# Attention and a top-1 mixture of experts in one Trainium2 kernel: gathered tokens take the same way through DVE's block transposes and DRAM as the hidden blocks

## Chip, cores and metric

The kernel runs on one core of one Trainium2 chip. The metric is the device time of one execution in microseconds (us); the number quoted for a kernel is the median of its runs.

## What is computed

The reference is a block-causal attention over 8 batches, 8 heads, 576 positions and head size 64 (blocks of 64; a query sees its own block and the earlier ones), whose output is laid out as x, 4608 tokens of 512. A gate matrix picks one of 8 experts for each token:

```python
logits = x @ w_gate
expert_idx = np.argmax(logits, axis=1)
gate_w = probs[np.arange(N), expert_idx]
for e in range(E):
    xe = x[expert_idx == e]
    h = np.maximum(xe @ w1[e], 0.0)      # 512 -> 1024
    out[expert_idx == e] = gate_w[...] * (h @ w2[e])   # 1024 -> 512
```

All data are float32. This change lies in the expert part alone.

## The kernel before

Attention runs first, and its tokens are written to a DRAM table `xd` (512 values and the gate weight in each row). The expert part then works in **slots** of 128 tokens that share an expert. With these inputs there are 38 slots (0 to 37), and the seven experts that get any tokens take 7, 9, 1, 4, 2, 3 and 12 of them, in this order: expert changes fall at slots 7, 16, 17, 21, 23 and 26. Slots 0 to 2 (`EARLY` = 3) are prepared specially; `period(t)` writes out the work of slot t from 2 on.

To keep float32's precision, TensorE multiplies in pieces: every operand is split into a high part (rounded, `xh`, `hh`, first half of `w`) and a low part (the rest, `xl`, `hl`), and a product is high*high + low*high + high*low. So `first_pe(t)` is 24 matmuls (two halves f of the 1024 hidden columns, 12 each), and `second_pe(t)` 24 more. PE's order in `period(t)` is `first_pe(t)`, the transposes of the next tokens (`rows_in(t + 1)`), `second_pe(t - 2)`.

- **Tokens.** `gather(t + 2)` (POOL, L881) fetches 128 rows by index into one of five buffers `xg`. `rows_in` (L899) turns them with four TensorE transposes into PSUM bank `px`; `rows_act` (L909, L912) has ACT copy `px` twice, as `xh` and `xf`, and `rows_pool` (L918) subtracts them to `xl`. There is one `xh` and one `xl`, so they may be written only when `first_pe(t)` is through.
- **Hidden blocks.** `relu_act` (L978) takes PSUM `ph` to `h`. `blocks` (L1015) has DVE transpose the 32 x 32 blocks of `h` into `hblk`; `leave` (L1022, a DMA issued by ACT) writes `hblk` to a DRAM buffer `there`, and `enter` (L1033, four DMAs) reads it back in another order, which completes the transpose, into `hp` (shown as `high` in the profile). `split_act` (L1044) makes `hh`, `split_pool` (L1054, two instructions) `hl`. These feed `second_pe` two periods later.
- **Weights.** SyncE loads the next expert's weights in eight chunks of 512 KB into four buffers `raw` (L1251, eight per expert), and DVE makes high and low parts from each: `units` (L1229 the high part, L1232 the low part). A table `pk`, worked out on the chip by `pieces`, says which of the four pieces (two chunks each, two CASTs and two subtractions) belong to a slot: an expert of one slot has all four of its successor's pieces in it, one of two slots has three and one, one of three has two, one and one, and longer ones have one in each of the first four slots. Pieces 0 and 1 (w1) run in period t, 2 and 3 (w2) in period t + 1. The weight memory holds two experts.
- **Order.** Each engine works through its own list, waiting on semaphores. In `period(t)` DVE has `blocks(t, 0)`, `blocks(t, 1)`, `units(t - 1, 1)`, `units(t, 0)`. ACT has `out_act`, `enter(t - 1)`, the two ReLUs, the two copies of `px`, `leave(t)`, `split_act(t - 1)`. `out_act` (L1100) scales by the gate weight, `out_pool` (L1106) scatters rows to the output.

## Time and profile before

| what | us |
| --- | --- |
| median of 3 runs (lowest, highest) | 847.27 (847.0, 852.77) |
| the profiled execution | 846.09 |
| its span, first to last instruction | 844.3 |
| outside the span | 1.8 |

Times in the profile count from the span's start. The expert part runs from about 377 us to the end. PE is TensorE's matmuls, PEld its weight loads, DVE VectorE, ACT ScalarE, POOL GpSimd, SP SyncE; ACTq and SPq are the queues' own instructions, among them the DMA issues. L-numbers are lines of the kernel before. first(17) stands for `first_pe(17)`, second(17) for `second_pe(17)`, hh(17) for the high part of slot 17's hidden block.

### The profile page before, as it was taken

To read this page: it belongs to the slowest core of one execution; us is meant where nothing else is said; L and a number is where in the kernel's file an instruction comes from. 1 tells how busy PE (TensorE), PEld (TensorE's weight loads), DVE (VectorE), ACT (ScalarE), POOL (GpSimd) and SP (SyncE) were. 2 spreads that over 40 slices of the span, in tenths; PEclk is the share of its full clock that TensorE was granted. 3 is DMA by queue.
4 is the path that set the end of the run, shared out by engine and by line. 5 is a ranking of instruction groups with operands and counts; after the bars stand their busy time and mean duration, and the time that the engine had idled before them with its cause. 6 is when DMAs were issued, how large, how long until landed. Compare 5 with 4: busy or idle time off the path is not lost.

```text
span 844.3 us, 16283 instructions
## 1 busy us (share of the span) xinstructions
PE 802.0 (95%) x4656; PEld 604.5 (72%) x4656; DVE 434.2 (51%) x1217; ACT 419.4 (50%) x1049; POOL 395.5 (47%) x394
## 2 busy tenths in 40 slices
PE   4999999999999999989999999989999999999993
PEld 2666677766666666667778888867788778888872
DVE  3567676767666667748445443135657771111100
ACT  3777677777777777734233333232232233333321
POOL 4112244434344623343666655553566575554452
PEclk9999999999999999999999999999999999999997
DMA  5229735455443538142466755446869854344440
GB/s 180 71 98 184 198 116 133 132 126 149 119 137 119 122 105 230 34 119 92 162 207 227 245 195 181 142 131 211 271 211 288 278 181 138 127 150 145 131 133 36
DMA packets 69248, 132.03 MB, mean 156 GB/s; under 512 B 10257, under 2 KB 31505, under 8 KB 69138
## 3 DMA queue, kind: packets, MB, share of 16 engines
q1 hardware_dynamic: 36418, 74.06, 30.8%
q10 hardware_dynamic: 25200, 36.71, 13.3%
q0 software_dynamic: 7520, 19.97, 7.2%
q8 instruction: 47, 0.77, 0.4%
q14 instruction: 63, 0.52, 0.2%
HBM read 90.91 MB, written 40.33 MB: 155 GB/s over the span
## 4 chain that ended last, share of the span: by engine, by line
PE 83%; issue 4%; DVE 4%; DMA 3%; POOL 2%; ACT 2%; DVEq 1%; ACTq 0%; POOLq 0%; SPq 0%
PE py L1083 21%; PE o L270 12%; PE ph L940 10%; PE o L940 10%; PE ya L169 7%; PE xa L169 4%; PE o L305 4%; PE px L899 1%; DMA raw<-w 1%; DMA there<-hblk 1%; PE o L299 1%; ACT pb L200 1%; PE o L158 1%; DVE w L1232 1%; POOL xl L918 0%
## 5 line engine op out<-in xcount | busy, mean ns | idle before, releaser
L1083 PE MATMUL py<-w,low 128*128 (+1 forms) x912 | 223.0, 399 | 1.7 <-issue 0.9
L1083 PEld LDWEIGHTS py<-w,low 128*128 128x128 f32 x912 | 168.1, 188 | 41.3 <-POOL low L1054 1.9
L1015 DVE STREAM_TRANSPOSE hblk<-h 128x512 f32<-128x512 f32 x70 | 48.9, 706 | 216.0 <-ACT h L978 135.3
L112 POOL TENSOR_SCALAR q<-qd 128x640 f32<-128x640 f32 x32 | 57.9, 1809 | 189.5 <-PE o L158 115.8
L1054 POOL TENSOR_TENSOR low<-high,low 128x512 fp32r<-128x512 f32 x70 | 101.8, 1474 | 32.1 <-ACT low L1044 32.1
L918 POOL TENSOR_TENSOR xl<-xf,xh 128x512 fp32r<-128x512 f32 x38 | 49.9, 1313 | 83.7 <-ACT xf L912 83.3
L940 PE MATMUL ph<-w,xh 128*128 x280 | 77.0, 397 | 6.1 <-DVE w L1229 4.2
L940 PE MATMUL o<-w,xh 128*128 x280 | 75.5, 391 | 0.0
L200 ACT ACTIVATE pb<-ya,neg 128x320 f32<-128x320 f32 (+2 forms) x96 | 50.0, 524 | 48.0 <-DVE neg L185 48.0
L1100 ACT ACTIVATE y<-py,xg 128x512 f32<-128x512 f32 x38 | 26.1, 686 | 92.8 <-PE py L1083 88.0
L1232 DVE TENSOR_TENSOR w<-raw,w 128x1024 f32 x48 | 70.1, 1499 | 0.0
L1106 POOL DMA_INDIRECT out<-y,idx x35 | 42.7, 1221 | 52.9 <-ACT y L1100 42.8
L978 ACT ACTIVATE h<-ph 128x512 f32<-128x512 f32 x37 | 22.1, 598 | 91.1 <-issue 52.4
L940 PEld LDWEIGHTS ph<-w,xh 128*128 128x128 f32 x280 | 53.0, 190 | 19.2 <-issue 7.2
L1229 DVE CAST w<-raw 128x1024 f32 x48 | 49.1, 1060 | 30.5 <-issue 22.2
L169 PE MATMUL ya<-kd,q 64*128 64x192 f32 (+2 forms) x192 | 61.8, 457 | 2.7 <-ACT pb L200 2.7
L169 PE MATMUL yb<-kd,q 64*128 64x192 f32 (+2 forms) x192 | 61.8, 456 | 0.0
L940 PEld LDWEIGHTS o<-w,xh 128*128 128x128 f32 x280 | 52.6, 188 | 11.4
L1044 ACT CAST low<-high 128x1024 fp32r<-128x1024 f32 x35 | 36.7, 1050 | 44.8 <-DVE hblk L1015 21.2
L697 POOL DMA_INDIRECT tab<-toks,posi x40 | 41.7, 1042 | 27.3 <-DVE run L664 13.8
L978 ACT ACTIVATE h<-o 128x512 f32<-128x512 f32 x37 | 22.1, 598 | 59.8 <-PE o L940 59.8
L200 ACT ACTIVATE pb<-yb,neg 128x192 f32<-128x192 f32 (+2 forms) x96 | 49.7, 525 | 0.4 <-DVE neg L185 0.4
(977 smaller groups left out, 1742.2 us busy)
## 6 DMA issues: line engine op xcount, KB each, us to landing
raw<-w SPq DMA_DIRECT2D x52, 512.0 KB
there<-hblk ACTq DMA_DIRECT2D x35, 512.0 KB, 3.1
high<-there ACTq DMA_DIRECT2D x140, 128.0 KB
qd<-qT SPq DMA_DIRECT2D x32, 352.0 KB, 3.2
v<-vt SPq DMA_DIRECT2D x32, 352.0 KB, 7.5
kd<-kT SPq DMA_DIRECT2D x32, 288.0 KB, 4.2
xd<-xt SPq DMA_DIRECT2D x7, 1026.0 KB
xd<-xg SPq DMA_DIRECT2D x9, 256.5 KB, 11.2
```

What stands on the lines that cost most here:

```text
L112: self.nc.gpsimd.tensor_scalar(q, self.raws[m][0][:, 0 : 512 + P], 0.125, None, ALU.mult)
L169: ins = mm(out, q[r, 128 * (i - 1) : 128 * i], k[r, o : o + n], start=True, stop=True, skip_group_check=True)
L200: ins = self.nc.scalar.activation(dst, src, AF.Exp, bias=self.neg[m][:, c : c + 1], scale=1.0, accum_out=self.sums[m][:, c : c + 1])
L270: self.nc.tensor.matmul(out[r], self.raws[m][2][:, slot], self.ph[m, bank][:, c0:c1], start=t in (0, 5), stop=t in (4, 5), skip_group_chec ...
L918: pool.tensor_sub(self.xl, self.xf, self.xh).then_inc(sem["xp"], 1)
L940: m = pe.matmul(self.ph[f], x[:, P * k : P * k + P], weights(k, f, part), start=start and k == 0, stop=stop and k == 3,)
L978: act.activation(self.h[f], self.ph[f], AF.Relu).then_inc(sem["ra"], 1)
L1015: dve.transpose(self.ht.rearrange("p (b f c i) -> p f c b i", b=4, f=2, c=4)[:, f], self.h[f].rearrange("p (c b j) -> p c b j", c=4, b=4), ...
L1054: pool.tensor_sub(self.hl[t % 2][:, f].rearrange("p (c a i) -> p c a i", c=4, a=4), inner(t)[:, f], self.hh[t % 2][:, f].rearrange("p (c a ...
L1083: m = pe.matmul(self.py[t % 2], h[:, c // 4, P * (c % 4) : P * (c % 4) + P], wf[:, bass.ds(off + (base + 512 * c), 512)], start=n == 0, st ...
L1229: dve.tensor_copy(part(c, 0), raw[c % 4]).then_inc(sem["wh"], 1)
L1232: dve.tensor_sub(part(c, 1), raw[c % 4], part(c, 0)).then_inc(sem["wd"], 1)
```

## The change

From slot 6 on (`EARLY + AHEAD`, with `AHEAD` = 3) the tokens no longer go through TensorE. DVE transposes the 32 x 32 blocks of slot t + 3's tokens into a third part of `hblk` along with slot t's hidden blocks; `there`, `hblk` and `hp` grow from 1024 to 1536 columns, and the DMAs carry 768 KB each way. On the far side ACT makes `xh` from `hp` (`apart_act`), POOL `xl` (`rows_pool`); the second copy `xf` is gone. Within `hblk` and `hp` the twelve column groups are now interleaved (a step of 12 elements, 48 bytes, between neighbours of a group), where a run of 32 neighbours was contiguous before. `xh`, `xl` and the PSUM banks `ph` are double (even slots use what were `pt0` and `pt1`); ReLU writes back into its PSUM bank and DVE reads it there. Six token buffers replace five, tokens are gathered four periods ahead instead of two, and the gate weight is copied out by DVE (`gates`), since the buffer is reused before the output is scaled. In a slot DVE now does its weight pieces first and the blocks afterwards, except where a new bit in `pk` ("late": position 0 or 1 within the expert's slots, and three or four pieces up to this slot) puts the blocks ahead. In the last slot DVE takes one of the two `hl` halves. In the start, `pieces` moves behind the first weight work, and `rows_pool(3)` ahead of `out_pool(0)`.

```diff
-XG = 5
+XG = 6
+AHEAD = 3
...
+        do(v.tensor_scalar(c[2], c[2], 1.0, None, ALU.is_le))
+        do(v.tensor_scalar(c[2], c[6], 2.5, c[2], ALU.is_gt, ALU.mult))
+        do(v.scalar_tensor_tensor(c[7], c[7], 2.0, c[2], ALU.mult, ALU.add))
...
+    def phs(self, t):
+        return self.pt if t > EARLY and t % 2 == 0 else self.ph
...
+        def apart_act(t):
+            act.wait_ge(sem["dr"], 64 * (t - AHEAD - EARLY + 1))
+            rows_free(act, t)
+            r, (xh, _) = apart(t)
+            act.copy(xh, r).then_inc(sem["xa"], 2)
...
-            act.activation(self.h[f], self.ph[f], AF.Relu).then_inc(sem["ra"], 1)
+            ph = self.phs(t)[f]
+            act.activation(self.h[f] if t < EARLY else ph, ph, AF.Relu).then_inc(sem["ra"], 1)
...
-            dve.transpose(
-                self.ht.rearrange("p (b f c i) -> p f c b i", b=4, f=2, c=4)[:, f],
-                self.h[f].rearrange("p (c b j) -> p c b j", c=4, b=4),
-            ).then_inc(sem["tb"], 1)
+            to = self.ht.rearrange("p (b i g) -> p g b i", b=4, g=12)
+            u = t + AHEAD
+            if u < NS:
+                dve.wait_ge(sg[u % XG], 16 * gathered(u))
+                rows = self.xg[u % XG]
+                dve.transpose(to[:, 8:12], rows[:, 0:DM].rearrange("p (k b j) -> p k b j", k=4, b=4)).then_inc(
+                    sem["tb"], 1
+                )
...
+            for f in range(2):
+                dve.wait_ge(sem["ra"], 2 * t + f - 1)
+                dve.transpose(
+                    to[:, 4 * f : 4 * f + 4], self.phs(t)[f].rearrange("p (c b j) -> p c b j", c=4, b=4)
+                ).then_inc(sem["tb"], 1)
...
+                if t + 1 < NS:
+                    act.wait_ge(sem["xp"], t + 1)
...
+            elif more and t + 1 >= EARLY + AHEAD:
+                apart_act(t + 1)
+            if more:
+                rows_pool(t + 1)
...
-            if more:
-                rows_in(t + 1)
-                rows_act(t + 1)
-                rows_pool(t + 1)
+            work(t)
             leave(t)
...
+        def work(t, old=True):
+            late = units(t - 1, 1, t) if old else None
+            units(t, 0)
+            if old:
+                with dve.If(late < 1):
+                    blocks(t)
+                dve.end_ifs()
```

DVE's list around slot 18 of the kernel before: the two block transposes, then the load of `pk` that opens the pieces, with their branches (`raw` and `w` are the weights).

```order
L1015 STREAM_TRANSPOSE hblk<-h_4962 128x4x4x32
L1015 STREAM_TRANSPOSE hblk<-h_4963 128x4x4x32
L1214 TENSOR_LOAD pk
L1214 ISA x2
L1221 REGISTER_ALU x3
L1221 COMPARE_AND_BRANCH
```

The same slot now opens with `pk`, and a branch on the late bit may put three transposes (tokens `xg`, then the two PSUM banks) and the gate's copy there; then come the pieces (left out).

```order
L1285 TENSOR_LOAD pk
L1285 ISA x2
L1294 REGISTER_ALU x2
L1294 COMPARE_AND_BRANCH
L1066 STREAM_TRANSPOSE hblk<-xg_194 128x4x128
L1072 COPY gates<-xg_194 128x1
L1078 STREAM_TRANSPOSE hblk<-pt_4967 128x4x128
L1078 STREAM_TRANSPOSE hblk<-pt_4968 128x4x128
L1294 UNCONDITIONAL_BRANCH
L1297 REGISTER_ALU x3
L1297 COMPARE_AND_BRANCH
```

Without the bit the same four instructions stand behind the last piece (rows at the end of slot 18).

```order
L1310 TENSOR_TENSOR w<-raw_84,w 128x1024
L1300 UNCONDITIONAL_BRANCH
L1319 COMPARE_AND_BRANCH
L1066 STREAM_TRANSPOSE hblk<-xg_194 128x4x128
L1072 COPY gates<-xg_194 128x1
L1078 STREAM_TRANSPOSE hblk<-pt_4967 128x4x128
L1078 STREAM_TRANSPOSE hblk<-pt_4968 128x4x128
L1319 UNCONDITIONAL_BRANCH
```

So the blocks move from ahead of a slot's pieces to behind them wherever the bit is 0. On ACT, a slot of the kernel before (`out_act`, `enter`, two ReLUs, two copies of `px`, `leave`, `split_act`):

```order
L1100 ACTIVATE y<-py_4970,xg_193 128x512
L1033 DMA high<-there_60 32x4x256 x4
L978 ACTIVATE h_4962<-ph_4965 128x512
L978 ACTIVATE h_4963<-o 128x512
L909 CAST xh<-px 128x512
L912 COPY xf<-px 128x512
L1022 DMA there_59<-hblk 128x1024
L1044 CAST low_78<-high 128x1024
```

and now:

```order
L1164 ACTIVATE y<-py_4970,gates 128x512
L947 CAST xh<-high 128x512
L1097 DMA high<-there_60 32x4x384 x4
L1025 ACTIVATE pt_4967<-pt_4967 128x512
L1025 ACTIVATE pt_4968<-pt_4968 128x512
L1083 UNCONDITIONAL_BRANCH
L1084 DMA there_59<-hblk 128x1536
L1111 CAST low_78<-high 128x1024
```

One copy remains of two, and it stands ahead of `enter`; `leave` and `split_act` keep their places, so hh(t - 1) still waits behind DVE's blocks of slot t.

## Rows read from the trace of the kernel before

**Rows 1.** The page's first part, the whole span: busy us (share of the span) and instructions of each engine.

```profile
PE 802.0 (95%) x4656; PEld 604.5 (72%) x4656; DVE 434.2 (51%) x1217; ACT 419.4 (50%) x1049; POOL 395.5 (47%) x394
```

**Rows 2.** The timeline late in the expert part, last expert, weight loads (PEld) around first(37): start us, duration us, engine, line, operation, tiles. L899 is the tokens' transposes, L1083 the second product, L940 the first.

```profile
801.00 5.43 PEld L1083 LDWEIGHTS py<-w,low 128*128 128x128 f32 x24
806.48 0.89 PEld L940 LDWEIGHTS ph<-w,xh 128*128 128x128 f32 x4
811.99 0.59 PEld L899 LDWEIGHTS px<-ident,xg 128*128 128x128 f32 x4
812.54 5.43 PEld L1083 LDWEIGHTS py<-w,low 128*128 128x128 f32 x24
```

**Rows 3.** The longest of PE's idle stretches from slot 3 on, from the timeline; in brackets the idle us in front of the instruction and what ended it.

```profile
409.30 1.20 PE L940 MATMUL ph<-w,xl 128*128 x4 [1.44 <-POOL xl L918]
427.16 1.18 PE L940 MATMUL ph<-w,xh 128*128 x4 [1.01 <-ACT xh L909]
570.80 1.51 PE L940 MATMUL ph<-w,xh 128*128 x4 [4.17 <-DVE w L1229]
603.99 4.00 PE L1083 MATMUL py<-w,low 128*128 x16 [0.45 <-POOL low L1054]
678.95 1.20 PE L940 MATMUL ph<-w,xh 128*128 x4 [0.93 <-ACT xh L909]
819.27 11.50 PE L1083 MATMUL py<-w,low 128*128 x48 [0.86 <-issue]
```

**Rows 4.** The stall at slot 17: the first half of first(17) and of first(22) in the chain that ended last (start us, us, count), and the window behind the stall (its us; busy time and count of PE, PEld, DVE, ACT, POOL; granted clock; DMA share; GB/s).

```profile
570.80 4.61 PE ph L940 x12
631.17 2.75 PE ph L940 x12
```

```profile
570.80:573.40 2.60, 2.60 (x8) 2.03 (x9) 2.12 (x2) 0.00 (x0) 0.12 (x1) 0.63 0.87 321
```

**Rows 5.** Timeline around slot 18, DVE, ACT and ACT's queue: L1229 the first CASTs of expert 4's pieces 2 and 3, L1015 slot 18's block transposes, L1022 `leave(18)`, L1044 hh(17).

```profile
584.84 1.30 DVE L1229 CAST w<-raw 128x1024 f32 x2 [5.31 <-PE py L1083]
...
597.48 1.30 DVE L1015 STREAM_TRANSPOSE hblk<-h 128x512 f32<-128x512 f32 x2
598.81 0.34 ACTq L1022 DMA_DIRECT2D there<-hblk  x1
599.25 1.06 ACT L1044 CAST low<-high 128x1024 fp32r<-128x1024 f32 x1 [7.96 <-DVE hblk L1015]
```

**Rows 6.** DVE's groups in 559 to 691 us (slots 16 to 26, eleven slots): busy us, mean ns of one, idle us in front and what ended it.

```profile
L1232 DVE TENSOR_TENSOR w<-raw,w 128x1024 f32 x30 | 43.5, 1487 | 0.0
L1229 DVE CAST w<-raw 128x1024 f32 x31 | 31.3, 1043 | 16.7 <-issue 8.4 <-PE py L1083 7.1 <-DMA raw<-w 1.2
L1015 DVE STREAM_TRANSPOSE hblk<-h 128x512 f32<-128x512 f32 x22 | 14.8, 696 | 38.5 <-ACT h L978 21.2 <-issue 17.3
```

**Rows 7.** The page's group of POOL's low halves; by form, a DVE reduction that reads 256 elements in steps of 8 elements; then, from the timeline, one that reads 128 neighbours in order (both make groups of 8).

```profile
L1054 POOL TENSOR_TENSOR low<-high,low 128x512 fp32r<-128x512 f32 x70 | 101.8, 1474 | 32.1 <-ACT low L1044 32.1
```

```profile
L577 DVE TENSOR_REDUCE L<-lg 128x32 f32<-128x256 f32 x8 | 4.9, 612 | 0.0
```

```profile
385.20 0.29 DVE L745 TENSOR_REDUCE few<-sums 128x16 f32<-128x128 f32 x1
```

**Rows 8.** The same stretch's middle, timeline of ACT, its queue and DVE: `leave(22)`, `enter(22)`, the block transposes of slot 23, `leave(23)`, hh(22).

```profile
644.37 0.34 ACTq L1022 DMA_DIRECT2D there<-hblk  x1
...
648.77 1.76 ACTq L1033 DMA_DIRECT2D high<-there  x4
...
651.27 1.31 DVE L1015 STREAM_TRANSPOSE hblk<-h 128x512 f32<-128x512 f32 x2 [2.39 <-ACT h L978]
...
652.61 0.34 ACTq L1022 DMA_DIRECT2D there<-hblk  x1
...
657.07 1.05 ACT L1044 CAST low<-high 128x1024 fp32r<-128x1024 f32 x1 [4.38 <-DMA high<-there]
```

**Rows 9.** DMA. A window in the loaded stretch (columns as in rows 4); ACT's queue (packets, MB, share of 16 engines) and the landing of `there` (KB each, median us) in 700 to 800 us, where no weights are loaded; the landing in 593 to 689 us.

```profile
629.00:641.00 12.00, 12.00 (x56) 9.77 (x55) 11.66 (x11) 3.90 (x6) 9.33 (x6) 1.00 0.88 265
```

```profile
q10 hardware_dynamic: 6394, 9.09, 28.1%
there<-hblk ACTq DMA_DIRECT2D x8, 512.0 KB, 2.8
```

```profile
there<-hblk ACTq DMA_DIRECT2D x9, 512.0 KB, 4.6
```

**Rows 10.** The start, timeline: first(3), the gather for slot 5, second(3); then the page's line of the gathers' DMA (count, median us from issue to landing).

```profile
406.55 0.88 PEld L940 LDWEIGHTS ph<-w,xh 128*128 128x128 f32 x4
414.10 0.99 POOL L881 DMA_INDIRECT xg<-xd,idx  x1 [0.27 <-POOL idx L877]
433.76 2.40 PEld L1083 LDWEIGHTS py<-w,low 128*128 128x128 f32 x11
```

```profile
xg<-xd,idx POOLq DMA_INDIRECT x37, 4.6
```

**Rows 11.** The end, timeline: `enter(37)`, hh(37), the weight loads of second(37) that waited for its low half.

```profile
817.22 2.54 ACTq L1033 DMA_DIRECT2D high<-there  x4
823.06 1.05 ACT L1044 CAST low<-high 128x1024 fp32r<-128x1024 f32 x1 [2.50 <-DMA high<-there]
826.76 3.57 PEld L1083 LDWEIGHTS py<-w,low 128*128 128x128 f32 x16 [0.21 <-POOL low L1054]
```

More of the change, by code (lines that the diff above doesn't have):

```diff
@@ L890, in gathered, with side @@
             return len([k for k in range(EARLY, t + 1) if k % XG == t % XG])
+        def side(t):
+            return 0 if t > EARLY and t % 2 == 0 else 1
         def rows_in(t):
@@ L903, in rows_in, with rows_free @@
             m.then_inc(sem["xt"], 1)
+        def rows_free(engine, t):
+            if t == EARLY + 1:
+                engine.wait_ge(sem["wh"], 8)
+            if t >= 2:
+                engine.wait_ge(sem["mm1"], 2 * t - 1 if t > EARLY else 2 * t + 1)
         def rows_act(t):
             act.wait_ge(sem["xt"], t)
-            if t >= 2:
-                act.wait_ge(sem["mm1"], 2 * t + 1)
-            act.copy(self.xh, self.px).then_inc(sem["xa"], 1)
+            rows_free(act, t)
+            act.copy(self.xh[side(t)], self.px).then_inc(sem["xa"], 1)
             if t >= 2:
@@ L962, in first_pe @@
                 if t >= EARLY:
-                    pe.wait_ge(sem["ra"], 2 * t + f - 3)
-                products(f, self.xh, 0, start=t >= EARLY)
-                for x, part, name, count in [(self.xl, 0, "xp", t), (self.xh, 1, "wd", e8 + 4)][: 1 if t < EARLY else 2]:
+                    free(f)
+                products(f, xh, 0, start=t >= EARLY)
+                for x, part, name, count in [(xl, 0, "xp", t), (xh, 1, "wd", e8 + 4)][: 1 if t < EARLY else 2]:
                     if f == 0:
@@ L1099, in out_act @@
                 act.wait_ge(sem["ga"], 48)
-            act.activation(self.y, self.py[t % 2], AF.Copy, scale=self.xg[t % XG][:, GATE : GATE + 1]).then_inc(
-                sem["ya"], 1
-            )
+            gate = self.xg[t][:, GATE : GATE + 1] if t < EARLY else self.gates[:, t : t + 1]
+            act.activation(self.y, self.py[t % 2], AF.Copy, scale=gate).then_inc(sem["ya"], 1)
         def out_pool(t):
@@ L1181, in period @@
                 split_act(t - 1)
-                split_pool(t - 1)
-            units(t - 1, 1)
-            units(t, 0)
+                for f in range(2):
+                    split_low(t - 1, f, pool)
             if t != EARLY + 1:
@@ L1193, in finish @@
             split_act(t)
-            split_pool(t)
+            for f in range(2):
+                split_low(t, f, (pool, dve)[f])
             for i in (t - 1, t):
-                second_pe(i, 0)
-                second_pe(i, 1)
+                second_pe(i, 0, i == t)
+                second_pe(i, 1, i == t)
             for i in (t - 1, t):
@@ L1204, in finish, with units @@
             for i in range(XG):
-                n = len([k for k in range(EARLY, min(last + 2, NS)) if k % XG == i])
+                n = len([k for k in range(EARLY, min(last + AHEAD + 1, NS)) if k % XG == i])
                 if n:
                     pool.wait_ge(sg[i], 16 * n)
-        def units(t, second):
-            pk = dve.value_load(self.pk[t : t + 1, 0:1], min_val=0, max_val=8 * 4096 - 1)
-            hi, lo, first, e8 = pk & 7, (pk >> 3) & 7, (pk >> 6) & 63, (pk >> 12) << 3
-            off = 16384 - (((pk >> 12) & 1) << 14)
+        def units(t, second, around=None):
+            pk = dve.value_load(self.pk[t : t + 1, 0:1], min_val=0, max_val=16 * 4096 - 1)
+            hi, lo, first, e8 = pk & 7, (pk >> 3) & 7, (pk >> 7) & 63, (pk >> 13) << 3
+            off = 16384 - (((pk >> 13) & 1) << 14)
             def part(c, j):
                 return wf[:, bass.ds(off + (4096 * (2 * (c // 4) + j) + 1024 * (c % 4)), 1024)]
+            late = (pk >> 6) & 1
+            if around is not None:
+                with dve.If(late > 0):
+                    blocks(around)
+                dve.end_ifs()
             with dve.If(hi > lo):
@@ L1226, in units @@
                                 dve.wait_ge(sem["mm2"], first + 1)
+                            else:
+                                dve.wait_ge(sem["mm1"], first * 2 + 1)
                             for c in (2 * i, 2 * i + 1):
@@ L1276, in run @@
             gather(EARLY)
+            gather(EARLY + 1)
             for k in range(4):
@@ L1286, in run @@
             dve.sem_inc(sem["me"], 1)
-            self.router.pieces(do, self.bank)
             for f in range(2):
@@ L1343, in attention_moe_kernel @@
     tab = dram.tile([P * TC, 1], I32, tag="tab", name="tab")
-    there = [dram.tile([P, 1024], F32, tag=f"there{i}", name=f"there{i}") for i in range(2)]
+    there = [dram.tile([P, 1536], F32, tag=f"there{i}", name=f"there{i}") for i in range(2)]
     rcst = ctx.enter_context(tc.tile_pool(name="rcst", bufs=1))
```

120 lines of the change are left out of this document (78 added, 42 removed).

## Prediction

> **What bounds the kernel now.** I read the page's busy shares first: PE works in 95% of the span, no other engine in more than 51% [rows 1]. So the question is what PE does that it need not do, and where it waits. The timeline of a late, quiet slot answers the first: from the second product's weight loads at 801.00 to the next at 812.54 a slot takes 11.54 us, and of that the tokens' transposes have the 0.55 us from 811.99 to 812.54; first and second product take 5.51 and 5.48 [rows 2]. The list of PE's idle stretches answers the second: one of 4.17 us at first(17), where the expert changes after a single slot and DVE's weight parts are late, and otherwise 0.3 to 1.4 us at the start, at slots 17, 23 to 26, and at the end [rows 3]. [...] Nearly everything else in the expert part is PE at its pace, and the chains beside it (DVE's blocks, the way through DRAM, hh) have slack. The change takes work from PE and puts it on those chains, so I go through the places where their slack is thin.
>
> **The transposes.** `rows_in` stays for slots 4 and 5 and goes for all later ones, up to the one for slot 38, which never runs. Counting the one for slot 6 to the start, 32 times 0.55 us [rows 2] fall away on PE: **17.6 us** gained, if the slot then takes 10.99. In a quiet slot I cost what comes instead at nothing: a third transpose of some 0.7 us on DVE, one copy on ACT in place of two, the same subtractions on POOL, DMAs half as long again. Their cover is a lag of two periods between first and second product. Where that cover is thin, they count, as follows. ReLU back into PSUM and DVE's reading from it have no row as such here; I cost both as the same instructions to SBUF.
>
> **Slot 17, expert 4's first.** DVE now takes the weight pieces ahead of the blocks. Expert 4's w1 pieces run in period 16 and no longer wait for ReLU(16), about one slot sooner, so the stall at first(17) goes: 6.1 gained, and the 0.45 of second(17) [rows 3] with it. But what is late next stands right behind. Pieces 2 and 3 of expert 4 wait for second(15), now 11.0 us after first(17) begins. From their first CAST to slot 18's blocks it was 597.48 - 584.84 = 12.6 [rows 5], the time of piece 0 of the next expert and of a wait for its DMA included. Slot 18's late bit is 0 (slot 17 has one piece), so piece 1 now comes ahead of its blocks as well: 2 x 1.04 + 2 x 1.49 = 5.1 [rows 6]. Then three transposes, 2.1, and hh(17), which stands behind `leave(18)` on ACT and ended 1.5 after the blocks (600.31 against 598.78) [rows 5]. That is 11.0 + 12.6 + 5.1 + 2.1 + 1.5 = 32.3. PE wants it after five half slots of 5.5, at 27.5: a new wait of 4.8, and 1.1 more for the low halves (two of 1.47 [rows 7] against 8 matmuls of 0.23). So 6.5 go and 5.9 come, and the clock may fall once more behind the new stall: I take **0** (bounds: 3 lost with the clock and a slower DMA, 6 gained if the weights land sooner).
>
> **Slots 18 to 26, four experts in ten slots.** In 559 to 691 us DVE is busy for 43.5 + 31.3 + 14.8 = 89.6 [rows 6]; eleven more transposes make it 97, of the 121 that PE would need. Not the sum but the ring is tight. Once blocks are late (up to three pieces, 15 us, stand ahead of slot 21's now), each slot's `leave` depends on the one before: landing, `enter`, ReLU on ACT behind it, the blocks, `leave`. That round was 652.61 - 644.37 = 8.2 us [rows 8], 3.3 less than a slot, so lateness shrank by that much a slot. Its DMA part, 4.4 (644.37 to 648.77 [rows 8]; median 4.6 there [rows 9]), grows by up to half, 2.2, with the bytes; the round becomes 10.4, and lateness shrinks by 0.6 a slot only. DMA is loaded too: 0.88 of 12 us in the window shown is 10.2 us of a slot; ACT's queue moved 9.09 MB in 28.1% of 100 us, 3.1 us a MB, so 0.52 MB more cost 1.6 and make 11.8, over the slot's 10.99 for three slots [rows 9]. Against this DVE starts its pieces up to a slot earlier. I take **5 lost** (bounds: none, if the head start covers all; 12, if each of four late slots costs 3).
>
> **The new layout.** Writes of the transposes and reads of hh, `xh` and the low halves go in steps of 48 bytes. The nearest rows are two DVE reductions: 612 ns for 256 elements in steps of 32 bytes, 290 ns for 128 in order, 2.4 and 2.3 ns an element [rows 7]. That is next to no price, so I take **0**. Upper bound: all go at 2.4 ns, a transpose 1.2 us instead of 0.7, hh 2.45 instead of 1.05. For POOL no row reads in steps. [...]
>
> **The start.** From first(3) to second(3) it was 433.76 - 406.55 = 27.2 [rows 10]. PE's work there is now first(3), second(2), first(4), first(5) of 5.5 each and two token transposes of 0.55: 23.1, to 429.7, since the waits at 409.30 and 427.16 [rows 3] go with `rows_pool` ahead of `out_pool` and tokens 5 ahead of first(4). But the first blocks now also wait for slot 6's tokens, whose gather stands behind that of slot 5: 414.10 + 1.4 = 415.5, landing 4.6 later [rows 10] at 420.1; transposes and gates 2.5; `leave` 0.3 and landing 2.8 x 1.5 = 4.2; `enter` to hh 5.8 as at the end [rows 11] and 0.8 for the bytes; hh 1.05. That is 434.8, 1 later than before, and half a us for the low half: **1.5 lost** (4 gained to 5 lost).
>
> **The end.** hh(37) comes 1.4 (half of 2.8 [rows 9]) and 0.8 later; PE had 0.7 of room in front of it (second(36) began at 819.27 and took 5.5, hh(37) ended at 824.1) [rows 3, 11]; the low half on two engines saves 0.2 [rows 11]. **1.5 lost** (0 to 4).
>
> **Sum.** 17.6 + 0 - 5 - 0 - 1.5 - 1.5 = 9.6 gained. The profiled execution took 846.09, 1.2 below the median of 847.27: 836.5 on its scale, **837.7** as a median.
>
> **Rivals.**
> - *Everything stays covered.* Pieces first take the stalls away and the ring keeps its lead. For it: DVE is idle for long stretches, 38.5 us in front of the blocks alone [rows 6]. Against it: the sum at slot 17, five us too late. It gives 17.6 + 6.1 + 2 at the start: 846.1 - 25.7, 821.6 as a median.
> - *The round becomes the bound: slower.* If steps of 48 bytes cost what the upper bound says, the round is 10.4 + 2 x 0.5 = 11.4, over the slot's 10.99, and lateness grows from slot to slot wherever weights are loaded; the point from which it decides is a transpose of 1.0. DVE then needs 89.6 - 14.8 + 33 x 1.2 = 114 and its 17 us of idle in front of CASTs [rows 6], 131 in all; with round and pieces in each other's way I put slots 17 to 27 at 13 us each, 22 over PE's 121. Then 846.1 - 17.6 + 22 + 3 + 4 (slot 17 with longer steps): 858.7 as a median. [...] The reductions of rows 7 do not agree.
> - *New stalls eat it all.* The lower bounds at half strength: 2 at slot 17, 9 in the stretch, 4 and 3 at start and end, 18 against 17.6: 847.7, no change. For it: the chain through slot 25 has no slack in the kernel before either, PE waits 0.93 at 678.95 [rows 3].
> - *Not as said.* `rows_in` is called for slots up to 5 alone, so PE's transposes do go; no chance is given to it.
>
> **How the numbers follow.** A measurement here tells about 1% from no change, 838.8 to 855.7. The forecast has 0.42, with 830 to 845 as its own spread: 0.25 below 838.8, 0.17 above. Everything covered: 0.24, all faster. Stalls eat it all: 0.18, the same. The round as bound: 0.16, of which 0.14 slower, 0.02 the same. So faster 0.49, same 0.37, slower 0.14. The range leaves out a tenth at each end: 822 to 853.
>
> **What would show it.** Right: 20 transposes on PE's token line instead of 152, quiet slots of 11.0 us; no idle time at first(17) but 4 to 6 us at second(17), released by ACT's hh; waits of second(20) to second(24) for hh or low, 5 us in all; block transposes of 0.7 us each, hh of 1.05. Wrong: transposes over 1.0 us or hh over 2 (the round), a slot of 11.0 that PE doesn't reach in the quiet stretch after slot 28, or no wait at second(17).

## The result and the profile after

| kernel | median us | ratio to the kernel before, 95% interval |
| --- | --- | --- |
| before, measured beside it | 849.62 | |
| changed | 855.07 | 1.0067 [1.0047, 1.0087] |

The change makes the kernel slower by 0.7%, where 1.1% faster was forecast. The profiled execution has a span of 854.6 us and a mean granted clock of 0.976; before it was 844.3 and 0.990.

The page's first part, the whole span of the changed kernel: busy us (share) and instructions of each engine, as in [rows 1].

```profile
PE 795.7 (93%) x4524; PEld 596.1 (70%) x4524; DVE 486.0 (57%) x1294; ACT 454.3 (53%) x1016; POOL 418.0 (49%) x397
```

PE has 132 matmuls fewer (the tokens' transposes of 33 slots) and 6 us less work in a span that is 10 us longer. So PE stands still more, or works slower; the next rows show both. The timeline of a quiet stretch, weight loads as in [rows 2] (L1146 second product, L988 first):

```profile
796.11 5.54 PEld L1146 LDWEIGHTS py<-w,low 128*128 128x128 f32 x24
801.69 5.53 PEld L988 LDWEIGHTS pt<-w,high 128*128 128x128 f32 x24
807.26 5.53 PEld L1146 LDWEIGHTS py<-w,low 128*128 128x128 f32 x24
```

A slot takes 11.15 here, and 11.12 on the mean of the eleven slots from second(24) to second(35), against 11.55: 0.43 less, not the 0.55 of the four transposes, because the 24 loads of the second product now take 5.54 where they took 5.43.

PE's idle stretches from slot 3 on, timeline, as in [rows 3], all above 0.3 us:

```profile
426.22 1.20 PE L988 MATMUL ph<-w,xl 128*128 x4 [0.38 <-POOL xl L953]
436.07 8.40 PE L1146 MATMUL py<-w,low 128*128 x24 [4.98 <-issue]
606.01 7.20 PE L1146 MATMUL py<-w,low 128*128 x24 [10.72 <-issue]
632.70 3.98 PE L1146 MATMUL py<-w,low 128*128 x16 [0.93 <-POOL low L1119]
643.48 2.13 PE L1146 MATMUL py<-w,low 128*128 x8 [1.24 <-issue]
646.48 3.99 PE L1146 MATMUL py<-w,low 128*128 x16 [0.87 <-POOL low L1119]
671.25 3.99 PE L1146 MATMUL py<-w,low 128*128 x16 [2.03 <-POOL low L1119]
683.42 7.47 PE L1146 MATMUL py<-w,low 128*128 x24 [2.68 <-issue]
824.87 5.86 PE L1146 MATMUL py<-w,low 128*128 x24 [0.54 <-issue]
833.91 7.41 PE L1146 MATMUL py<-w,low 128*128 x24 [3.19 <-issue]
```

In order these are first(5), second(3), second(17), second(19), second(20) twice, second(22), second(23), second(36) and second(37). The stall at first(17) is gone. Nine of the ten now stand at a second product, where the kernel before had one such wait above 0.5 us. At three of them POOL's low half ends the wait. At five, second(3), (17), (20), (23) and (37), PE starts 0.2 to 0.3 us after ACT ended hh, so hh ends it. What second(36) waits for (0.54) isn't shown. Read the second number too: 24 matmuls take 5.86 at 824.87, but 8.40, 7.20, 7.47 and 7.41 behind the four longest waits, 7 us more in all. The windows behind three of them (columns as in [rows 4]) show why: the granted clock is 0.64 to 0.79, a mean of two levels (0.50 of full in 438 to 439 us, 1.00 in 442 to 443), after PE had been idle for 3.2 to 10.7 us.

```profile
436.00:444.00 8.00, 7.93 (x23) 6.28 (x24) 6.41 (x9) 1.96 (x3) 5.79 (x5) 0.64 0.99 262
606.00:612.00 6.00, 5.99 (x20) 4.83 (x21) 3.17 (x4) 2.49 (x4) 5.68 (x5) 0.75 0.58 139
833.00:841.00 8.00, 7.09 (x24) 5.61 (x24) 1.07 (x1) 1.21 (x2) 3.38 (x2) 0.79 0.10 36
```

What lies on the way to hh, the groups by form in 400 to 855 us (busy us, mean ns of one, idle in front and its releaser; to be read against [rows 6] and [rows 7]):

```profile
L1119 POOL TENSOR_TENSOR low<-high,low 128x512 fp32r<-128x512 f32 x69 | 116.9, 1715 | 139.0 <-ACT low L1111 137.7 <-PE py L1146 1.2
L1111 ACT CAST low<-high 128x1024 fp32r<-128x1024 f32 x35 | 72.0, 2057 | 139.6 <-DMA high<-there 70.5 <-DVE hblk L1078 64.2 <-PE py L1146 5.0
L1066 DVE STREAM_TRANSPOSE hblk<-xg 128x512 f32<-128x512 f32 x35 | 39.2, 1121 | 109.0 <-DMA there<-hblk 66.3 <-DMA xg<-xd,idx 40.8 <-issue 1.8
L1078 DVE STREAM_TRANSPOSE hblk<-pt 128x512 f32<-128x512 f32 x34 | 35.8, 1096 | 28.9 <-ACT pt L1025 28.9
```

A block transpose takes 1.10 us instead of 0.70, hh 2.06 instead of 1.05, a low half 1.72 instead of 1.47. All three go in steps of 48 bytes now.

For an account, the start of the weight loads of second(t) in each timeline divides the expert part into stretches. Each row is one profiled execution, in us. Take them with care: the kernel before was profiled in a quick execution (846.09, its median beside the change is 849.62) and the change in one a little above its median (856.42), so the rows differ by 11.9 where the medians differ by 5.5. And where two kernels have the same code in a stretch, as runs 6 and 7 up to slot 4 or runs 1 and 6 in slots 18 to 23, the rows differ by up to 1.6.

| kernel | second(2) to (4) | (4) to (14) | (14) to (18) | (18) to (24) | (24) to (35) | (35) to end | sum |
| --- | --- | --- | --- | --- | --- | --- | --- |
| before | 30.96 | 115.47 | 53.01 | 71.75 | 127.02 | 31.76 | 429.97 |
| changed | 36.92 | 111.54 | 57.22 | 77.65 | 122.28 | 36.25 | 441.86 |
| 1, runs of 32 | 34.69 | 111.60 | 54.71 | 73.22 | 122.58 | 34.84 | 431.64 |
| 2, blocks first | 36.86 | 111.20 | 62.21 | 75.05 | 122.57 | 36.36 | 444.25 |
| 3, before with steps | 30.96 | 115.47 | 58.07 | 75.97 | 127.01 | 34.11 | 441.59 |
| 4, before with 768 KB | 30.99 | 115.48 | 54.01 | 83.53 | 127.02 | 33.98 | 445.01 |
| 5, as 1, slot 18 blocks first | 35.91 | 111.46 | 50.50 | 71.95 | 123.04 | 33.83 | 426.69 |
| 6, as 1, start | 33.00 | 113.81 | 54.49 | 71.83 | 123.04 | 34.55 | 430.72 |
| 7, both of these | 31.42 | 112.27 | 49.47 | 76.85 | 123.05 | 34.29 | 427.35 |
| 8, as 1, hh(17) first | 35.71 | 111.48 | 54.30 | 76.72 | 122.26 | 33.39 | 433.86 |
| 9, as 1, blocks between pieces | 32.02 | 111.86 | 52.03 | 76.02 | 122.27 | 33.74 | 427.94 |
| 10, before, extra issue | 31.00 | 115.48 | 53.95 | 74.63 | 127.02 | 32.78 | 434.86 |
| 11, before, wide reads | 30.97 | 115.48 | 57.17 | 76.81 | 127.03 | 33.37 | 440.83 |
| 12, as 7, short rides | 34.84 | 111.18 | 48.59 | 68.86 | 122.57 | 31.52 | 417.56 |

In the long stretches, slots 4 to 13 and 24 to 34, the change gains (3.9 and 4.7 us). It loses 6.0 at the start, 4.2 around slot 17, 5.9 in slots 18 to 23 and 4.5 at the end.

### The profile page after: what moved, and what is told of

Read it like the earlier page. It is cut to its first block, busy times and chain, and to the rows that moved or that the text cites. A ratio compares the mean times of both kernels' runs of the same rounds, so it can differ in the third digit from the quotient of the medians.

```text
span 854.6 us, 16182 instructions
## 1 busy us (share of the span) xinstructions
PE 795.7 (93%) x4524; PEld 596.1 (70%) x4524; DVE 486.0 (57%) x1294; ACT 454.3 (53%) x1016; POOL 418.0 (49%) x397
## 4 chain that ended last, share of the span: by engine, by line
PE 73%; issue 10%; DMA 6%; POOL 4%; DVE 3%; ACT 2%; DVEq 1%; ACTq 1%; POOLq 0%; SPq 0%
PE py L1146 18%; PE o L270 12%; PE pt L988 7%; PE ya L169 7%; PE xa L169 4%; PE o L988 4%; PE ph L988 4%; PE o L305 4%; DMA there<-hblk 2%; DMA high<-there 1%; PE o L299 1%; ACT pb L200 1%; DVE hblk L1078 1%; POOL tab L698 1%; DMA xg<-xd,idx 1%
## 5 line engine op out<-in xcount | busy, mean ns | idle before, releaser
L1146 PE MATMUL py<-w,low 128*128 (+1 forms) x912 | 228.0, 406 | 27.2 <-issue 23.3
L1146 PEld LDWEIGHTS py<-w,low 128*128 128x128 f32 x912 | 175.5, 194 | 73.3 <-issue 25.9
L1119 POOL TENSOR_TENSOR low<-high,low 128x512 fp32r<-128x512 f32 x69 | 116.9, 1715 | 139.0 <-ACT low L1111 137.7
L1111 ACT CAST low<-high 128x1024 fp32r<-128x1024 f32 x35 | 72.0, 2057 | 139.6 <-DMA high<-there 70.5
L1066 DVE STREAM_TRANSPOSE hblk<-xg 128x512 f32<-128x512 f32 x35 | 39.2, 1121 | 109.0 <-DMA there<-hblk 66.3
L988 PE MATMUL pt<-w,high 128*128 x408 | 97.8, 395 | 0.0
L988 PEld LDWEIGHTS pt<-w,high 128*128 128x128 f32 x408 | 76.7, 188 | 18.3 <-issue 0.3
L1078 DVE STREAM_TRANSPOSE hblk<-pt 128x512 f32<-128x512 f32 x34 | 35.8, 1096 | 28.9 <-ACT pt L1025 28.9
L895 POOL DMA_INDIRECT xg<-xd,idx x39 | 44.5, 1142 | 10.8 <-POOL idx L887 10.5
L169 PE MATMUL xa<-kd,q 64*128 64x288 f32 x128 | 41.1, 443 | 6.5 <-POOL q L112 6.5
L305 PE MATMUL o<-fold,oT 128*128 128x144 f32 x256 | 43.9, 294 | 1.1 <-ACT oT L277 0.6
L185 DVE TENSOR_REDUCE neg<-yb 128x1 f32<-128x192 f32 (+2 forms) x96 | 42.8, 473 | 3.3
L1164 ACT ACTIVATE y<-py,gates 128x512 f32<-128x512 f32 x35 | 24.1, 689 | 34.4 <-PE py L1146 22.2
```

Source lines behind the costliest of these rows:

```text
L169: ins = mm(out, q[r, 128 * (i - 1) : 128 * i], k[r, o : o + n], start=True, stop=True, skip_group_check=True)
L305: mm(t[:, i], self.oT[m, 0][:, o : o + P], w, start=True, stop=True)
L895: pool.indirect_dma_start(out=self.xg[i], out_offset=None, in_=self.xd[:, :], in_offset=bass.IndirectOffsetOnAxis(ap=self.idx[:, t : t + 1 ...
L988: m = pe.matmul(ph[f], x[:, P * k : P * k + P], weights(k, f, part), start=start and k == 0, stop=stop and k == 3,)
L1111: act.copy(hh, h).then_inc(sem["hn"], 1)
L1119: engine.tensor_sub(hl[:, c], h[:, c], hh[:, c]).then_inc(sem["ln" if engine is pool else "le"], 1)
```

## The experiments

Theories. L: the layout in steps of 48 bytes is what the forecast missed. O: DVE's order (pieces first) is. D: the bytes of the rides are. From the fifth run on, Q: hh(t - 1) waits in ACT's list behind `leave(t)`, and that behind pieces on DVE; its rival B: what order gives back, the bytes take in slots 18 to 23. Ratios are to the kernel before on the same chip, with 95% intervals. Diffs are cut (`...`), semaphore counts and sizes that follow from an edit above all. The expectations count by another list: their eighth run is run 7 here.

**1. Contiguous runs of 32** in `hblk`, `there` and `hp`, nothing else.

```diff
-            to = self.ht.rearrange("p (b i g) -> p g b i", b=4, g=12)
+            to = self.ht.rearrange("p (b g i) -> p g b i", b=4, g=12)
...
-            r = self.hp[(t - AHEAD) % 2].rearrange("p (m g) -> p g m", g=12)[:, 8:12]
+            r = self.hp[(t - AHEAD) % 2].rearrange("p (a g i) -> p g a i", a=4, g=12)[:, 8:12]
...
```

> The changed kernel with one edit: in hblk, there and hp the twelve column groups lie in runs of 32 neighbours again, in place of steps of 12 elements; all else as changed. Theory L (the stepped layout is what the forecast missed: block transposes 1.11 us against 0.71 before, hh 2.06 against 1.05, xh 1.14): transposes back to 0.70, hh to 1.05, xh to 0.6, the waits of second(3) and second(17) about half of 5.0 and 10.7, the end's 3.2 below 1.5; time 838 to 844. Theory O (DVE's pieces ahead of the blocks are what costs): the durations fall, but the wait at second(17) stays over 7 and the time stays within 4 of 855. Theory D (the bytes of the longer rides): waits stay where hh waits for its DMA, time above 848.

Measured: 848.19, 0.997 [0.9947, 0.9994]; against the change's 1.0067 that is 1.0%, some 8 us. Its groups, 400 to 847 us:

```profile
L1119 POOL TENSOR_TENSOR low<-high,low 128x512 fp32r<-128x512 f32 x69 | 97.1, 1426 | 136.0 <-ACT low L1111 136.0
L1111 ACT CAST low<-high 128x1024 fp32r<-128x1024 f32 x35 | 36.8, 1050 | 127.4 <-DMA high<-there 77.1 <-DVE hblk L1078 50.3
L1066 DVE STREAM_TRANSPOSE hblk<-xg 128x512 f32<-128x512 f32 x35 | 24.8, 709 | 116.3 <-DMA there<-hblk 88.1 <-DMA xg<-xd,idx 26.2 <-issue 1.8
L1078 DVE STREAM_TRANSPOSE hblk<-pt 128x512 f32<-128x512 f32 x34 | 22.8, 698 | 32.3 <-ACT pt L1025 32.3
```

The durations are those of before again, though ReLU and DVE use PSUM as in the change. The steps cost, and PSUM does not (a transpose takes 698 ns out of it, 696 from SBUF in [rows 6]). Theory L holds for the durations and the sign; but 848 is above its 838 to 844, and the waits at second(3), second(17) and the end shrink less than it said. The wait of 7.58 at second(17) is as O said (over 7), the time just over 848 as D said. So more was missed than the layout. The four longest waits that remain:

```profile
436.48 7.38 PE L1146 MATMUL py<-w,low 128*128 x24 [4.35 <-issue]
602.01 8.15 PE L1146 MATMUL py<-w,low 128*128 x24 [7.58 <-issue]
651.45 2.12 PE L1146 MATMUL py<-w,low 128*128 x8 [1.58 <-issue]
825.32 7.41 PE L1146 MATMUL py<-w,low 128*128 x24 [2.14 <-issue]
```

**2. Blocks first** in every slot, in the change's own layout.

```diff
-            late = units(t - 1, 1, t) if old else None
-            units(t, 0)
             if old:
-                with dve.If(late < 1):
-                    blocks(t)
-                dve.end_ifs()
+                blocks(t)
+                units(t - 1, 1)
+            units(t, 0)
```

> The changed kernel, stepped layout and all, but DVE always does a slot's blocks ahead of its weight pieces, as in the kernel before (the late bit is not asked). Theory O: the wait of 10.7 at second(17) goes, time below 847. Theory L: that wait goes, the stall at first(17) of about 4 us with its slow clock comes back, the start's and the end's waits stay; time 848 to 854. Theory D: nothing but slot 17 moves, 850 to 855.

Measured: 859.54, 1.0102 [1.0048, 1.0156], against the change's 1.0067, with intervals that overlap. PE waits 7.51 us at first(17), where the pieces come late again, and 4.58 at second(17). Theory O falls: blocks first are no faster, the stall at first(17) comes back, and 4.58 of the 10.72 at second(17) stay beside it. The time lies above the ranges of all three theories, L's 848 to 854 too; L, like O, had second(17)'s wait gone.

**3. The kernel before with its eight groups in steps of 32 bytes.**

```diff
-                self.ht.rearrange("p (b f c i) -> p f c b i", b=4, f=2, c=4)[:, f],
+                self.ht.rearrange("p (b i f c) -> p f c b i", b=4, f=2, c=4)[:, f],
...
-            return self.hp[t % 2].rearrange("p (a f c i) -> p f c a i", a=4, f=2, c=4)
+            return self.hp[t % 2].rearrange("p (m f c) -> p f c m", f=2, c=4)
...
```

> The kernel before with one edit: the eight column groups of hblk, there and hp interleaved in steps of 8 elements, 32 bytes. Theory L: block transposes about 1.1 us, hh about 2.0; in slots of 11.54 us most of it is hidden, but the waits for hh and low halves in slots 17 to 26 grow, 851 to 858. Theories O and D: the chain has slack for it, within 3 of the kernel before.

Measured: 861.4, 1.0131 [1.008, 1.0181]. Steps alone (of 32 bytes here), without the change, cost 11 us; the time lies above L's 851 to 858. Its groups, 400 to 855 us:

```profile
L1015 DVE STREAM_TRANSPOSE hblk<-h 128x512 f32<-128x512 f32 x70 | 82.9, 1201 | 199.6 <-ACT h L978 192.6 <-POOL low L1006 7.0
L1044 ACT CAST low<-high 128x1024 fp32r<-128x1024 f32 x35 | 78.1, 2232 | 60.6 <-DVE hblk L1015 47.6 <-DMA high<-there 13.0
```

**4. The kernel before with rides of 768 KB**, the added 256 KB in a second write, a copy of the first 512 columns that nobody uses.

```diff
-            act.dma_start(self.there[t % 2], self.ht).then_inc(sem["dw"], 16)
+            to = self.there[t % 2].rearrange("p (b r) -> p b r", b=4)
+            act.dma_start(to[:, :, 0:256], self.ht.rearrange("p (b r) -> p b r", b=4)).then_inc(sem["dw"], 16)
+            act.dma_start(to[:, :, 256:384], self.ht[:, 0:512].rearrange("p (b r) -> p b r", b=4)).then_inc(sem["dw"], 16)
...
```

> The kernel before with the rides' bytes of the changed one: each slot writes 768 KB to DRAM (in two DMAs, 512 and 256 KB, the second a copy of columns that are not used) and reads 768 KB back in four. Theory D: the waits in slots 17 to 26 grow to some 8 us together, 853 to 860. Theory L and theory O: the longer landing is mostly hidden, 848 to 853.

Measured: 863.88, 1.014 [1.0085, 1.0196], some 12 us; in the account 11.8 of 15.0 lie in slots 18 to 23. That is above D's range, and the run has an extra issue and smaller packets beside the bytes (in 593 to 689 us 10848 on ACT's queue for 10.23 MB, in the kernel before 5898 for 8.92); runs 10 to 12 part these.

**5. As 1, and in slot 18 alone the blocks ahead of the pieces.**

```diff
-            late = units(t - 1, 1, t) if old else None
+            ahead = old and t in (18,)
+            if ahead:
+                blocks(t)
+            late = units(t - 1, 1, None if ahead else t) if old else None
...
-            if old:
+            if old and not ahead:
```

> The changed kernel with contiguous runs of 32 (as in the first experiment), and the blocks ahead of the pieces in slot 18 alone. Theory Q (ACT's queue: hh(17) waits behind leave(18), and that for blocks which DVE does behind ten CASTs and ten subtractions): leave(18) at about 587 instead of 600, hh(17) behind it, the wait of 7.6 us at second(17) under 1 and the 2.3 us of slow clock behind it gone: 838 to 842. Rival B (the bytes of the rides are the limit: slots 18 to 23 only have more room because PE stood still at 17): the waits of slots 18 to 23, 4.6 us with contiguous runs, grow by what slot 17 gives back: 845 to 849.

Measured: 845.23, 0.9951 [0.9924, 0.9979]. The wait at second(17) falls from 7.58 to 1.55, with 2.28 for a low half behind it, and the slow clock stays (16 matmuls in 5.55 instead of 3.99):

```profile
594.34 0.34 ACTq L1084 DMA_DIRECT2D there<-hblk  x1
594.77 1.05 ACT L1111 CAST low<-high 128x1024 fp32r<-128x1024 f32 x1 [10.78 <-DVE hblk L1078]
596.02 2.12 PE L1146 MATMUL py<-w,low 128*128 x8 [1.55 <-DVE w L1307]
600.42 5.55 PE L1146 MATMUL py<-w,low 128*128 x16 [2.28 <-POOL low L1119]
```

The profile names weights (DVE w) for the 1.55. But PE starts 0.20 behind the end of hh(17) at 595.82, as it does at every second product that waits for hh, so hh ended this wait too. `leave(18)` goes at 594.34 and not at Q's 587, since the pieces of slot 17's period still stand ahead of the blocks. The account shows 4.2 us gained from slot 14 to 18, in an execution of 841.8. By the ratios the gain on run 1 is 0.2%, with intervals that overlap, and the median misses Q's 838 to 842. It is in B's 845 to 849, but slots 18 to 23 did not grow as B had it.

**6. As 1, start:** the gathers of slots 5 and 6 ahead of slot 2's second low half, and slot 3's blocks ahead of its pieces.

```diff
-                for f in range(2):
-                    hidden_low(t, f, pool)
+                hidden_low(t, 0, pool)
                 gather(EARLY + 2)
                 gather(EARLY + 3)
+                hidden_low(t, 1, pool)
...
```

> The changed kernel with contiguous runs; in the start the gathers of slots 5 and 6 go ahead of the second low half of slot 2, and the blocks of slot 3 ahead of its pieces. Theory Q: leave(3) some 3 us earlier, the wait at second(3) 4.4 -> 1 to 1.5, with a us of the slow clock: 843.5 to 846. Rival (the wait at second(3) is DRAM's way, landing and enter, whatever the gather does): wait stays over 3.5, time 847 to 849.

Measured: 847.76, 0.994 [0.9915, 0.9964]. second(3) waits 2.40 (for hh again) and 1.62 for a low half in place of 4.35; the transposes that wait for slot 6's tokens begin 5.1 us behind second(2)'s start and not 7.6, and hh(3) ends 2.2 us sooner. The account has 1.7 us gained up to slot 4, about what two rows of the same code differ by, and given back by slot 14. Q's 843.5 to 846 is missed. The time is in the rival's 847 to 849 and the two waits together, 4.02, are over its 3.5; but hh does come sooner with the gather, which the rival denied.

**7. Both.**

> Both together: contiguous runs, blocks first in slots 3 and 18, gathers 5 and 6 earlier. Theory Q: the two gains add, 833 to 838, faster than the kernel before by 1.3 to 2%. Rival B: 840 to 846.

Measured: 844.68, 0.9931 [0.9904, 0.9958]; faster than before, but the gains don't add to Q's 833 to 838; it is in B's 840 to 846. Start and slot 17 keep theirs, and slots 18 to 23 take 76.85 where run 1 took 73.22. The new stall is at second(20): DVE's last pieces, blocks of slot 21, ACT's hh(20), PE.

```profile
630.85 2.35 DVE L1310 TENSOR_TENSOR w<-raw,w 128x1024 f32 x2
633.12 0.70 DVE L1066 STREAM_TRANSPOSE hblk<-xg 128x512 f32<-128x512 f32 x1
635.55 1.04 ACT L1111 CAST low<-high 128x1024 fp32r<-128x1024 f32 x1 [11.72 <-DVE hblk L1078]
636.80 7.41 PE L1146 MATMUL py<-w,low 128*128 x24 [3.87 <-issue]
```

**8. As 1, and in slot 18 ACT does hh(17) ahead of `leave(18)`.**

```diff
-            leave(t)
+            if t != 18:
+                leave(t)
             if t > EARLY:
                 split_act(t - 1)
+            if t == 18:
+                leave(t)
```

> The changed kernel with contiguous runs and DVE's order as in the change; in slot 18 alone ACT does hh(17) ahead of leave(18). Theory Q: hh(17) at about 585, no wait at second(17) (under 0.5); but leave(18) stays at 600, so hh(18) at about 610 to 611 is late for second(18), which PE reaches at 605.5: the wait moves one slot on, 4 to 6 us there, 845 to 849. Rival (second(17) waits for the weight parts, not for hh): the wait of 7.6 us stays at second(17).

Measured: 849.34, 0.9975 [0.995, 0.9999], as run 1, and just above Q's 845 to 849. ACT, DVE and PE around slot 18:

```profile
588.13 1.05 ACT L1111 CAST low<-high 128x1024 fp32r<-128x1024 f32 x1 [3.60 <-DMA high<-there]
594.85 5.76 PE L1146 MATMUL py<-w,low 128*128 x24
601.36 0.71 DVE L1066 STREAM_TRANSPOSE hblk<-xg 128x512 f32<-128x512 f32 x1
605.33 7.39 PE L988 MATMUL pt<-w,high 128*128 x24 [4.72 <-ACT high L947]
615.54 4.81 PE L1146 MATMUL py<-w,low 128*128 x12 [2.82 <-issue]
```

second(17) no longer waits, so it was hh and not the weights (the rival). What follows is late all the same: slot 20's rows (made by `apart_act`, which stands behind `leave(18)`) and then hh(18), 7.5 us together where the wait was 7.6. The stall belongs to the late blocks, and order on ACT only says where it is paid.

**9. As 1, blocks between a slot's two sets of pieces, gathers of slots 5 and 6 earlier still.** `units(t, 0, ...)` has `blocks(t)` at its head unless the late bit is set or the slot carries all four pieces.

```diff
-            late = units(t - 1, 1, t) if old else None
-            units(t, 0)
-            if old:
-                with dve.If(late < 1):
-                    blocks(t)
-                dve.end_ifs()
+            if not old:
+                units(t, 0)
+            elif t == EARLY:
+                blocks(t)
+                units(t - 1, 1)
+                units(t, 0)
+            else:
+                units(t, 0, None, units(t - 1, 1, t))
```

> The changed kernel with contiguous runs, and DVE's blocks between a slot's two sets of pieces: behind those of the slot before, ahead of its own, except in a slot that carries all four pieces (16), where all pieces stay ahead; slot 3's blocks first; the gather of slot 5 among the first ones and that of slot 6 ahead of both low halves of slot 2. Theory Q (hh(t - 1) stands behind leave(t), and that behind three pieces): the waits at second(17) (7.6 us with contiguous runs alone), second(20) (3.9 in the eighth run) and second(3) (4.4) shrink to under 2 each, with less slow clock behind them: 837 to 842. Rival B (what order gives back, the bytes of the rides take in slots 18 to 24): 843 to 847.

Measured: 845.43, 0.9882 [0.9835, 0.993], the time of run 7, in B's 843 to 847 and above Q's 837 to 842. second(20) no longer waits, but second(17) (3.32), second(21) (1.82) and second(23) (3.74) do, each until 0.2 us after its hh.

**10. The kernel before with a second, tiny DMA behind each `leave`.**

```diff
...
+            act.dma_start(to[0:4, :, 256:384], self.ht[0:4, 0:512].rearrange("p (b r) -> p b r", b=4)).then_inc(sem["dw"], 16)
```

> The kernel before with a second, very small DMA (16 packets of 512 bytes) issued by ACT behind each leave, the big one in packets of 1 KB as in the fourth run, no more bytes read. It takes the 256 KB more each way out of that run and leaves its extra issue. Theory D (the bytes cost): 849 to 853, as before. Rival (the extra issue on ACT and the second landing cost): 857 to 864, as the fourth run.

Measured: 854.6, 1.002 [0.9991, 1.0049]: no difference shown. D's 849 to 853 is missed, but the kernel before took 853.52 beside it. The issue is not what run 4 paid for.

**11. The kernel before with only the reads widened** to 768 KB (the added columns are written once per buffer).

> The kernel before with 768 KB read by each enter (four DMAs of 192 KB) and 512 KB written by each leave: half of the fourth run's bytes and no extra issue. Theory D (the bytes cost): 854 to 859, landing of high longer, waits at second(19) to second(23). Rival (extra issue): 849 to 852.

Measured: 860.61, 1.0062 [1.003, 1.0095], some 5 us: half of run 4's bytes, somewhat under half of its cost. The time is above D's 854 to 859, but so was the kernel before above its other medians (853.52). Theory D holds in the kernel before.

**12. As 7, with rides of 512 KB.** The tokens' columns are not carried, so from slot 6 on the products are made of what lies in their place: this run is for its time alone, and its output is not the kernel's.

```diff
-            act.dma_start(self.there[t % 2], self.ht).then_inc(sem["dw"], 16)
+            to, ht = (x.rearrange("p (b r) -> p b r", b=4)[:, :, 0:256] for x in (self.there[t % 2], self.ht))
+            act.dma_start(to, ht).then_inc(sem["dw"], 16)
...
-            view = self.there[t % 2].rearrange("(a j) (b r) -> b j a r", a=4, b=4)
+            view = self.there[t % 2].rearrange("(a j) (b r) -> b j a r", a=4, b=4)[:, :, :, 0:256]
...
```

> The eighth run (contiguous runs, blocks first in slots 3 and 18, gathers earlier), in which the way out and the way back carry the hidden blocks alone, 512 KB as in the kernel before, in packets of 1 KB; the tokens' third stays behind, so from slot 6 on the products are made of what lies in its place. All instructions stay. Theory D (in the changed kernel too the bytes of the rides cost): the six slots from second(18) to second(24), 76.9 us in the eighth run, fall to 67 to 71, start and end by 1 each: 832 to 839. Rival (the order of DVE's pieces, blocks and ACT's leave sets these slots, whatever the bytes): over 74 there, 842 to 846.

Measured: 834.43, 0.9797 [0.9765, 0.9829]; against run 7 that is 1.3%, 11 us. Landings in 593 to 689 us, run 7 and then this run (KB each, median us):

```profile
there<-hblk ACTq DMA_DIRECT2D x8, 768.0 KB, 5.3
high<-there ACTq DMA_DIRECT2D x32, 192.0 KB, 4.6
```

```profile
there<-hblk ACTq DMA_DIRECT2D x9, 512.0 KB, 4.6
high<-there ACTq DMA_DIRECT2D x32, 128.0 KB, 3.7
```

Slots 18 to 23 fall from 76.85 to 68.86 (PE's own pace is 6 x 11.12 = 66.7), the end by 2.8. D's 67 to 71 there and its 832 to 839 are hit. The end gains more than the 1 it said, and the start loses 3.4 (34.84 against 31.42), since second(3) waits as in run 6. So in the changed kernel, too, what order gave back in one place the bytes took in the next: that is why run 7's gains don't add, and the likely reason for runs 5, 6, 8 and 9, which were not run without the bytes. Runs 5, 6, 7 and 9, with whole rides, beat the kernel before by 0.5 to 1.2%, and do not differ clearly among themselves.

## Why the prediction was wrong

The step that failed is **the new layout**: "That is next to no price, so I take **0**". Its upper bound was near (transpose 1.2 forecast, 1.10 measured; hh 2.45 and 2.06). Run 1 puts the price at some 8 us by the ratios (10.2 in the account: 2.2 at the start, 2.5 around slot 17, 4.4 in slots 18 to 23, 1.4 at the end). Without it the change would be no slower than the kernel before. The value was taken from the reductions of [rows 7], 2.4 ns an element in steps and 2.3 in order. But the operations in question are faster than that: a transpose of 512 elements takes 0.70 us, 1.4 ns an element, a CAST of 1024 takes 1.05, 1.0 ns. So the row of a slower instruction did not show what a step costs these; the upper bound, which took 2.4 ns an element for all of them, was the nearer reading (2.1 and 2.0 measured).

In these runs ACT's read doubles with steps of 48 and 32 bytes (1050 to 2057 and 2232 ns for 1024 elements), and a block transpose that writes in such steps takes 0.4 to 0.5 us more. For POOL the forecast had no row in steps. Measured, its low half went from 1426 ns in run 1 to 1715 in the change, a fifth more, so some 0.6 us a waiting place of two halves.

The other steps:

- *Transposes, 17.6 gained.* They are gone, as said (20 are left on PE's token line). But a slot fell by 0.43, so 33 slots gave 14.2. The term was over-sized by 3.4.
- *Slot 17, 0.* The mechanism was right in every link: no stall at first(17), DVE's pieces ahead of slot 18's blocks, hh(17) behind `leave(18)`. The sum was 32.3 us from first(17)'s start to hh(17)'s end, and the change took 39.0 (566.80 to 605.81):

```profile
579.24 1.30 DVE L1307 CAST w<-raw 128x1024 f32 x2 [1.70 <-PE py L1146]
580.46 5.14 POOL L1119 TENSOR_TENSOR low<-high,low 128x512 fp32r<-128x512 f32 x2 [1.76 <-ACT low L1111]
584.11 4.02 DVE L1307 CAST w<-raw 128x1024 f32 x2
...
597.03 1.29 DVE L1307 CAST w<-raw 128x1024 f32 x2 [2.30 <-issue]
598.24 2.35 DVE L1310 TENSOR_TENSOR w<-raw,w 128x1024 f32 x2
600.51 1.05 DVE L1066 STREAM_TRANSPOSE hblk<-xg 128x512 f32<-128x512 f32 x1
601.44 1.94 DVE L1078 STREAM_TRANSPOSE hblk<-pt 128x512 f32<-128x512 f32 x2
603.41 0.34 ACTq L1084 DMA_DIRECT2D there<-hblk  x1
603.84 1.97 ACT L1111 CAST low<-high 128x1024 fp32r<-128x1024 f32 x1 [19.03 <-DVE hblk L1078]
```

  The first CAST is 12.5 behind first(17)'s start (11.0 forecast), the next slot's pieces start 17.8 behind that (12.6), and the rest takes 8.8 (8.7: these pieces are 1.6 shorter, blocks and hh 1.7 longer by the layout). The 17.8 has two parts that no term had. Three pieces end at 594.73, 15.5 after the first CAST, where before they took 12.7: two CASTs take 4.02 beside POOL's subtractions, and 1.29 at 597.03 without them. Then DVE stands 2.30, with the table's load and the branches in its list. So the wait is 10.7 and not 4.8, and 1.4 of slow clock follow, which the forecast named and left in the bounds. The 6.1 that it counted for the stall at first(17) is 4.2 of idle time [rows 3] and 1.9 by which 12 matmuls are longer there than at first(22) [rows 4]; the change has neither (no wait in front of 567.03, and 12 matmuls from there to 569.77, in 2.74).
- *Slots 18 to 26, 5 lost.* second(18) to second(24) takes 5.9 more where 6 x 0.43 = 2.6 less was due: 8.5 lost, inside the bounds; 4.4 of it is layout. The waits came at second(20), (22) and (23), as foreseen, and at second(19), and the clock added 1.6. Runs 4, 11 and 12 show that the bytes cost there, as the DMA terms of the sum had it; how much of the rest is theirs in the change's own order no run parts.
- *Start, 1.5 lost.* 6.0, past the bound of 5: 2.2 layout, 2.6 slow clock behind the wait of 4.98 at second(3).
- *End, 1.5 lost.* 4.5, past the bound of 4: the wait is 3.19 and the clock takes 1.6 behind it; 1.4 is layout.

So the sum of 9.6 gained turned into a loss (5.5 by the medians, 10.3 between the profiled executions, from which these parts are taken) by four things: 8 to 10 for the layout, some 3 of transposes that were not there to gain, some 5 on DVE's list at slot 17 (run 1 has 3.6 of it, the layout the rest), and 7 us of slow clock behind four waits, which was in no term but only in a bound (run 1 still has 5.4 of it: 7.38, 8.15 and 7.41 against 5.84; so 1.6 counts in the layout's part too). The time came out near the 858.7 of the rival on the slower side, and its condition, a transpose of 1.0 or more, was met. Its mechanism is half right, and the near time is in part luck: slots 18 to 23 took 12.9 each, where it said 13 for eleven slots, but the round was not above a slot. `leave` to `leave` took 7.9 to 10.9 us, except in slots 21 and 24, where three pieces stood ahead of the blocks (19.1 and 20.6). The chance of 0.16 was too small, above all since the 1.0 us at which this rival decides lay inside the 0.7 to 1.2 that the forecast itself gave a transpose.

## What to carry to other kernels

When a change puts a tile's elements in steps, price it for the engines' fastest instructions and not by a slow one (here a CAST went from 1.0 to 2.0 ns an element, where a reduction at 2.4 showed nothing); if no row shows it, take the upper bound as a likely case. Work that leaves the busiest engine for a way through DRAM can pay in bytes: here a third fewer of them made run 12 faster than run 7 by 11 us, 8.0 of it in slots 18 to 23, where weights load, and in runs 7 to 9 a better order mostly moved the wait. Price each new wait of a few us on TensorE with the slow clock behind it (1.4 to 2.6 us here, behind waits of 2.7 to 10.7).
